# Key weights loaded in their natural layout and turned on TensorE, feature weights by rows, warm-ups between the first steps, and a new order of the first half, in a fused attention and Mish kernel

## Chip, cores and metric

One core of one Trainium2 chip runs the whole program. The metric is device time in microseconds, median of several executions. A profiled execution adds a trace of every engine: TensorE (PE, with its weight loads PEld), VectorE (DVE), ScalarE (ACT), GpSimd (POOL) and SyncE (SP), whose queue issues most DMAs.

## The reference

```python
def _A_ref(x, wqkv, w_phi, wo):
    B, S, D = x.shape
    H = 32; Dh = D // H
    qkv = (x @ wqkv).reshape(B, S, 3, H, Dh).transpose(2, 0, 3, 1, 4)
    q, k, v = qkv[0], qkv[1], qkv[2]
    pq = jnp.einsum("bhsd,hdf->bhsf", q, w_phi)
    pk = jnp.einsum("bhsd,hdf->bhsf", k, w_phi)
    phi_q = jnp.concatenate([_softmax(pq, axis=-1), _softmax(-pq, axis=-1)], axis=-1)
    phi_k = jnp.concatenate([_softmax(pk, axis=-1), _softmax(-pk, axis=-1)], axis=-1)
    kv = jnp.einsum("bhsf,bhsd->bhfd", phi_k, v)
    z  = jnp.einsum("bhsf->bhf", phi_k)
    num = jnp.einsum("bhqf,bhfd->bhqd", phi_q, kv)
    den = jnp.einsum("bhqf,bhf->bhq", phi_q, z)[..., None] + 1e-6
    return (num / den).transpose(0, 2, 1, 3).reshape(B, S, D) @ wo

def _B_ref(x, w1, b1, w2):
    h = jnp.einsum("bsd,df->bsf", x, w1) + b1
    sp = jnp.log1p(jnp.exp(-jnp.abs(h))) + jnp.where(h > 0, h, jnp.zeros_like(h))
    return jnp.einsum("bsf,fd->bsd", h * jnp.tanh(sp), w2)

xn = _layernorm(A_x, axis=-1)
return A_x + _A_ref(xn, A_wqkv, A_w_phi, A_wo) + _B_ref(xn, B_w1, B_b1, B_w2)
```

S is 2048 tokens, D 512, F 1792; 32 heads of 16. All inputs are bf16.

## The kernel before

Tokens are cut into 16 tiles of 128, four tiles to a group. A token tile is normalised (statistics `LS`, `LN`; root `RS`; centring `AZ`, `AP`), then turned so that features lie on partitions (xnT). The first group is turned on TensorE (`TP`, kept by `TC`), tile by tile; the others by DMA transposes on SP's queue.

The key projection and the feature weights w_phi are folded into one matrix: the key weights are turned (wT), multiplied by a block-diagonal form of w_phi (Wbd, made by `WB` from wsrc and the 0/1 pattern `block`), and the four products (`F0`) are copied into wkp (`FD`). wkp therefore holds first the natural key weights and then the folded ones. After it come logits (`LP` for the first two tiles, `L`, `WL`, copied by `LC`), values (`V`, `VC`), extremes (`E`), exponentials (`X`), sums (`S`), the reciprocals and products (`R`, `N`) and the accumulation of kv (`A`). The hidden layer of the Mish branch runs as 56 units `H` (four groups by 14 blocks of 128 features), each followed by its activation `M`. The second half has queries (`Q`, `G`, `C`), the second layer (`O`, `P`) and the output (`Y`).

Before, the key weights arrive in two ways: rows 0 to 255 by a natural load into wkp (L522), to be turned on TensorE by matmuls against the identity into fp32 banks (`TW`, L616; copied by `TK`, L622), and rows 256 to 511 by a transposing DMA straight into wT (L523). w_phi comes by a load whose runs are one row of 16 features long (L528). Twelve dummy matmuls (L554) run on TensorE before the first step.

The order of everything is written by hand as a string, STEPS, at line 24. Each step is a name with arguments; `@b` is the PSUM bank, `a`, `v` and `p` name ACT, VectorE or POOL. An engine runs its instructions in the order in which the steps issue them; a wait holds all that is behind it on that engine. There are six banks of 512 fp32, and a step that writes a bank waits until its last tile has been read. Mish on ACT uses another table than exponential and logarithm, so changing between them costs a table load (L139).

Of the kernel before, what the change touches and what calls it, by code (L numbers as in the profile page):

```python
# [8 lines left out]
BF16 = mybir.dt.bfloat16  # L9
# [3 lines left out]
ALU = mybir.AluOpType  # L13
# [15 lines left out]
2 @4; M 2; H 3 @5; H 4 @0; H 5 @2; VC 0 a; H 6 @1; M 3; M 4; M 5; H 7 @4; M 6; M 7; H 8 @3; H 9 @5;  # L29
H 10 @0; M 8; H 11 @2; H 12 @1; LN 1; M 9; E 0 0; AP 1 0; AP 1 1; H 13 @4; L 1 0 @3; DX 3; L 1 3 @5;  # L30
DW 2; E 0 1; X 0 1; LN 2; LC 1 0 v; LC 1 3 v; WL 1; LN 3; AP 2 0; AP 2 1; X 0 0; V 6 @3; M 10; M 11;
M 12; H 14 @5; S 0 0; WL 2; LC 1 2 a; VC 6 a; H 17 @2; H 16 @0; M 14; AP 3 0; AP 3 1; H 15 @3; M 17;
M 13; H 18 @1; M 15; H 20 @5; H 19 @4; M 20; LC 1 1 v; H 22 @2; M 16; WT; H 21 @0; M 18; H 26 @5; S
0 1; M 19; H 24 @3; H 27 @0; H 23 @5; M 21; M 26; H 25 @1; M 22; M 23; E 1 0; E 1 1; M 24; M 25; H
28 @4; H 29 @3; L 2 0 @2; M 28; L 2 1 @5; LC 2 0 v; M 27; F @4,3; L 2 2 @1; LC 2 1 v; M 29; R 0 0 a;
FC 1 v; FC 0 v; L 2 3 @0; FC 2 a; FC 3 a; L 3 0 @5; R 0 1 a; L 3 2 @3; V 7 @1; FT 0; LC 2 2 a; V 9
@0; FT 1; N 0 0; LC 2 3 v; X 1 1; E 2 0; V 3 @2; DW 3; X 1 0; A 0 0; VC 3 a; VC 9 a; L 4 0 @4; LC 3
0 a; V 2 @2; VC 7 a; V 8 @0; VC 8 a; VC 2 a; N 0 1; E 2 1; LC 4 0 v; L 3 3 @5; LC 3 3 a; LC 3 2 a; V
4 @0; A 0 1; VC 4 a; L 4 2 @1; X 2 0; V 11 @5; S 1 1; S 1 0; S 2 0; L 4 3 @3; VC 11 a; L 3 1 @0; L 4
1 @5; LC 3 1 a; LC 4 1 a; H 31 @0; LC 4 2 a; H 30 @5; V 5 @1; R 1 0 a; LC 4 3 v; M 30; VC 5 a; H 32  # L40
@4; M 31; M 32; R 1 1 v; H 33 @2; M 33; N 1 1; H 34 @1; H 35 @3; H 36 @5; M 34; H 37 @0; M 35; H 38
@4; E 3 0; H 39 @2; H 40 @1; M 36; N 1 0; M 37; M 38; M 39; H 41 @3; H 42 @5; H 43 @0; M 40; A 1 0;
M 41; E 3 1; M 42; M 43; A 1 1; X 2 1; V 12 @4; VC 12 a; L 5 0 @2; V 10 @1; V 15 @3; VC 15 a; V 13
@5; V 14 @0; E 4 0; E 4 1; LC 5 0 a; VC 13 v; VC 10 a; L 5 2 @4; X 3 1; X 3 0; L 6 3 @3; VC 14 a; L
5 3 @2; O 0 @5; LC 5 2 a; S 2 1; S 3 1; S 3 0; R 3 1 a; R 2 1 a; N 2 1; R 2 0 a; L 6 0 @1; R 3 0 a;
N 3 0; L 5 1 @0; LC 5 1 a; N 3 1; O 1 @4; L 6 1 @0; LC 6 0 a; LC 6 3 a; L 6 2 @1; H 44 @3; X 4 0; N
# [16 lines left out]
def kernel(  # L63
# [12 lines left out]
    nc = tc.nc  # L76
    P = 128
# [15 lines left out]
    wphi_v = A_w_phi.rearrange("(j i) a b -> (i a) j b", j=4)  # L93
# [18 lines left out]
    wsrc = wts.tile([P, 4, DH], BF16, name="wsrc")  # L112
    wv = wts.tile([P, KT, D], BF16, name="wv")
# [8 lines left out]
    ident = consts.tile([P, P], BF16, name="ident")  # L122
    mhalf = consts.tile([P, TPG], FP32, name="mhalf")
# [9 lines left out]
    tables = ["natural_log_exp_and_others"]  # L133
# [11 lines left out]
    pf_of = {}  # L145
# [28 lines left out]
    def centre(out, xs, mv, rstd):  # L174

        nc.vector.tensor_scalar(
            out=out, in0=xs, scalar1=mv[:, 0:1], scalar2=rstd, op0=ALU.subtract, op1=ALU.mult
        )
# [105 lines left out]
    def take(s, i, copy):  # L284
        if i == 0:
            p_of[s] = smx.tile([P, TPG, 512], BF16, name="p_sb")
        copy(p_of[s][:, i, :], pl_of.pop((s, i)))  # L287
# [229 lines left out]
    for t in range(2):  # L517
        nc.sync.dma_start(x_sb[:, t, :], x_v[:, t, :])


    wT_of = {0: lnp.tile([P, 4, 512], BF16, name="wT", tag="xn")}
    nc.sync.dma_start(wkp[:, 0:2, :], wqkv_v[:, 0:2, D : 2 * D])  # L522
    nc.sync.dma_start_transpose(  # L523
        out=wT_of[0][:, :, 2 * P : 4 * P], in_=A_wqkv[2 * P : 4 * P, D : 2 * D]
    )
    nc.scalar.dma_start(b1b[:], b1_v[:, :])
    with nc.allow_non_contiguous_dma(reason="tiny w_phi load"):
        nc.scalar.dma_start(wsrc[:], wphi_v)  # L528
    nc.sync.dma_start(x_sb[:, 2:4, :], x_v[:, 2:4, :])
    nc.sync.dma_start(wv[:], wqkv_v[:, :, 2 * D : 3 * D])  # L530
    nc.sync.dma_start(w1_sb[:, :, 0 : 7 * P], w1_v[:, :, 0 : 7 * P])
    nc.sync.dma_start(x_sb[:, 4:8, :], x_v[:, 4:8, :])
    nc.sync.dma_start(w1_sb[:, :, 7 * P : F], w1_v[:, :, 7 * P : F])

    nc.scalar.preload_act_table_set(tables[0])
    make_identity(nc, ident[:])

    nc.gpsimd.memset(block[:], 1.0)
# [6 lines left out]
    nc.gpsimd.memset(mhalf[:], -0.5)  # L545
    nc.gpsimd.memset(eps[:], 1e-5)
# [12 lines left out]
    for n in (512,) * WARM + (P,) * SHORT:  # L559
        dummy(n)  # L560

# [5 lines left out]
    def weights_by_block():  # L567
        nc.vector.tensor_tensor(
            out=Wbd[:].rearrange("p j (h e) -> p j h e", h=8),
            in0=block[:, None, :, :].to_broadcast([P, 4, 8, 16]),  # L570
            in1=wsrc[:, :, None, :].to_broadcast([P, 4, 8, 16]),
            op=ALU.mult,
        )
# [19 lines left out]
    def first_root(i, on):  # L593
        _, mv, rstd = ln_of[0]
        r = rstd[:, i : i + 1]
        if on == "a":
            nc.scalar.activation(r, mv[:, i, 1:2], ACT.Ln, bias=eps[:])
# [123 lines left out]
```

## Time and profile before

| | |
|---|---|
| Median of 3 runs | 173.83 us (173.5 to 173.9) |
| Profiled execution, its own time | 173.62 us |
| Span of the profile, first to last instruction | 171.9 us |
| TensorE busy | 168.3 us in 1047 matmuls |
| VectorE, ScalarE, GpSimd busy | 146.0, 122.2, 7.9 us |
| HBM read, written | 7.10 MB, 2.10 MB |

A line of a timeline has start, duration, engine, line, operation, tiles (out<-in), the number merged, and in brackets the idle time before it and what ended it. A line of the chain of waits has start, duration and the work that set the end at that moment. A DMA line has tiles, queue, number, size and the median time from issue to landing. A matmul's duration holds its way through the array, so the pace of a row of matmuls is read from the chain, where they do not overlap.

### The profile page before, as it was taken

What the parts mean: (1) busy time and instruction counts of PE and PEld (TensorE: products, weight loads), DVE (VectorE), ACT (ScalarE), POOL (GpSimd) and SP (SyncE); (2) the same over time, 40 slices, a digit from 0 to 9 for tenths busy, and PEclk for the clock granted to TensorE, in tenths of its full rate; (3) what the DMA queues carried; (4) which work ended last, traced back from release to release, by engine and by line L of the source; (5) the groups of instructions that cost most, each with busy time, mean ns of one, the idle gap of its engine ahead of it and who ended that gap; (6) DMA issues with size and microseconds to landing.
All of it is one profiled execution on the core that took longest, in us unless ns stands there. A gap on an engine that the chain in (4) does not pass through costs nothing.

```text
span 171.9 us, 2743 instructions
## 1 busy us (share of the span) xinstructions
PE 168.3 (98%) x1047; PEld 82.5 (48%) x1047; DVE 146.0 (85%) x226; ACT 122.2 (71%) x196; POOL 7.9 (5%) x23
## 2 busy tenths in 40 slices
PE   8999999999999999999999999999999999999993
PEld 3754444444445544454445644544444444554452
DVE  3769998999899999999989999899799998884333
ACT  2778899976998979799978989978282792432200
POOL 4122102300000000000000000000000000000000
PEclk9999999999999999999999999999999999999999
DMA  4997199686064000000000194309345628778641
GB/s 119 299 374 253 33 217 356 147 162 126 4 115 129 0 4 0 0 0 0 4 0 0 40 111 97 63 15 142 91 107 110 150 59 190 155 161 206 91 124 61
DMA packets 46297, 18.55 MB, mean 108 GB/s; under 512 B 38092, under 2 KB 46284, under 8 KB 46284
## 3 DMA queue, kind: packets, MB, share of 16 engines
q1 hardware_dynamic: 45584, 18.26, 45.8%
q10 hardware_dynamic: 700, 0.12, 0.4%
q8 instruction: 8, 0.13, 0.3%
q14 instruction: 5, 0.04, 0.1%
HBM read 7.10 MB, written 2.10 MB: 53 GB/s over the span
## 4 chain that ended last, share of the span: by engine, by line
PE 98%; DVE 0%; issue 0%
PE ph L263 28%; PE po L497 28%; PE pl L229 14%; PE po L504 8%; PE pv L229 8%; PE warm L554 3%; PE pnd L452 2%; PE pkv L421 2%; PE pl L244 1%; PE pwide L229 1%; PE pfold L151 1%; PE ptw L616 1%; PE ptr L609 1%; PE pfold L203 0%; DVE x_sb L511 0%; PE pb L577 0%
## 5 line engine op out<-in xcount | busy, mean ns | idle before, releaser
L497 PE MATMUL po<-w_sb,acts 128*128 128x512 bf16 (+2 forms) x238 | 50.8, 366 | 0.0
L263 PE MATMUL ph<-xnT,w_sb 128*128 128x512 bf16 x224 | 50.1, 379 | 0.0
L274 ACT ACTIVATE acts<-ph,b1f 128x512 bf16<-128x512 f32 x56 | 35.9, 694 | 5.4 <-PE ph L263 5.4
L340 DVE TENSOR_REDUCE s<-e 128x128 f32<-128x2048 bf16 x16 | 36.1, 2277 | 0.5 <-ACT e L323 0.5
L263 PEld LDWEIGHTS <-w_sb 128*128 128x128 bf16 x224 | 21.7, 98 | 25.9 <-issue 0.3
L497 PEld LDWEIGHTS <-acts 128*128 128x128 bf16 x238 | 22.1, 98 | 23.6
L323 ACT ACTIVATE e<-e 128x2048 bf16<-128x2048 bf16 x16 | 30.4, 1917 | 0.0
L229 PEld LDWEIGHTS <-xnT 128*128 128x128 bf16 x184 | 17.6, 98 | 20.3 <-issue 0.2
L511 DVE TENSOR_TENSOR x_sb<-po,x_sb 128x512 bf16<-128x512 f32 (+2 forms) x17 | 11.0, 656 | 8.4 <-PE po L504 8.4
L504 PE MATMUL po<-wqk,xnT 128*128 128x512 bf16 (+2 forms) x68 | 15.6, 366 | 0.0
L229 PE MATMUL pl<-wqk,xnT 128*128 128x512 bf16 x64 | 15.6, 379 | 0.0
L229 PE MATMUL pv<-wv,xnT 128*128 128x512 bf16 x64 | 15.4, 379 | 0.0
L287 ACT CAST p_sb<-pl 128x512 bf16<-128x512 f32 x21 | 11.9, 590 | 4.1 <-PE pl L229 4.0
L467 ACT COPY ds<-pnd 128x32 f32<-128x32 f32 x16 | 2.9, 183 | 16.5 <-PE pnd L452 16.5
L139 ACT ACT_TABLE_LOAD x10 | 12.8, 1283 | 0.2
L298 DVE TENSOR_TENSOR m<-m 128x512 bf16<-128x512 bf16 (+1 forms) x32 | 11.5, 358 | 1.1
L229 PE MATMUL pl<-wkp,xnT 128*128 128x512 bf16 x48 | 11.5, 379 | 0.0
L165 DVE BATCH_NORM_STATS2 stats<-x_sb 128x6 f32<-128x512 bf16 x16 | 10.1, 678 | 1.3 <-DMA x_sb<-in_A_x_dram 1.3
L298 DVE TENSOR_TENSOR m<-p_sb 128x1024 bf16<-128x1024 bf16 x16 | 10.9, 682 | 0.1
L307 DVE TENSOR_TENSOR e<-p_sb,m 128x2048 bf16<-128x2048 bf16 x8 | 9.8, 1225 | 0.4 <-PE pkv L421 0.2
L374 DVE TENSOR_TENSOR e<-e,r 128x2048 bf16<-128x2048 bf16 x8 | 9.6, 1219 | 0.6 <-ACT r L349 0.5
L307 DVE TENSOR_TENSOR e<-m,p_sb 128x2048 bf16<-128x2048 bf16 x8 | 9.8, 1226 | 0.3
(73 smaller groups left out, 134.0 us busy)
## 6 DMA issues: line engine op xcount, KB each, us to landing
w_sb<-in_B_w_dram SPq DMA_DIRECT2D x4, 896.0 KB, 8.0
out_dram<-x_sb SPq DMA_DIRECT2D x15, 128.0 KB, 2.0
x_sb<-in_A_x_dram SPq DMA_DIRECT2D x3, 512.0 KB, 8.0
wv<-in_A_wqkv_dram SPq DMA_DIRECT2D x1, 512.0 KB, 5.1
wqk<-in_A_wo_dram SPq DMA_DIRECT2D x1, 512.0 KB
x_sb<-in_A_x_dram SPq DMA_DIRECT2D x2, 128.0 KB, 2.1
wkp<-in_A_wqkv_dram SPq DMA_DIRECT2D x1, 256.0 KB, 3.5
x_sb<-in_A_x_dram SPq DMA_DIRECT2D x1, 256.0 KB, 3.5
```

Of the source, the lines that this page charges most:

```text
L139: nc.scalar.preload_act_table_set(name)
L229: nc.tensor.matmul(pp, lhsT=xnT[:, t, kt, :], rhs=w(kt), start=(kt == 0), stop=(kt == KT - 1),)
L263: nc.tensor.matmul(ph_of[u][:], lhsT=w1_sb[:, kt, f * P : (f + 1) * P], rhs=xnT[:, g * TPG : (g + 1) * TPG, kt, :], start=(kt == 0), stop= ...
L274: nc.scalar.activation(acts[:, f, g * 512 : (g + 1) * 512], ph_of.pop(u)[:], ACT.Mish, bias=b1f[:, f : f + 1])
L287: copy(p_of[s][:, i, :], pl_of.pop((s, i)))
L298: nc.vector.tensor_tensor(out=m[:], in0=src[:, :, 0:half], in1=src[:, :, half : 2 * half], op=op)
L307: nc.vector.tensor_tensor(out=e_of[s][:].rearrange("p t j l c -> p (t j) l c")[:, :, pl, :].rearrange("p t (c e o) -> p t c e o", e=8, o=2 ...
L323: nc.scalar.activation(v, v, ACT.Exp)
L340: nc.vector.reduce_sum(t[:], pair(s, k).rearrange("p t j l (c e) -> p (t j l c) e", e=16), axis=AX.X)
L497: nc.tensor.matmul(po_of[t, c.stop][:, c], lhsT=acts[:, f, t * P : (t + 1) * P], rhs=w2_sb[:, f, c], start=(f == 0), stop=False,)
L504: nc.tensor.matmul(po_of[t, c.stop][:, c], lhsT=oT_of[t // 2][:, t % 2 * 4 + j, :], rhs=wo_sb[:, j, c], start=False, stop=(j == 3),)
L511: nc.vector.tensor_tensor(out=y, in0=po_of.pop((t, c.stop))[:, c], in1=y, op=ALU.add)
```

## The change

The tables of the first steps are written anew, up to step `A 1 1`; behind it the order is the same, with other bank numbers. The parts:

- Both halves of the key weights come by natural loads into wkp (`D wn02`, `D wn24`), ahead of the second token tile in SP's queue; the transposing load is gone. All four quarters are turned on TensorE (`TW 0` to `TW 3`), by transposes into bf16 banks instead of matmuls into fp32 banks. `TK 0`, `TK 2`, `TK 3` copy on VectorE, `TK 1` on ACT.
- w_phi comes by rows, 128 bytes to a partition (wraw), and is spread to its place by 16 matmuls of 16 columns with a selector `sel` as weights (`WX`), which is then copied to wsrc (`WC`). The selector is written on VectorE and POOL into space that kvm uses later. The load is the first on ACT's queue, the bias load the second.
- `WB` runs on POOL instead of VectorE. Fills of ident, block, eps and mhalf are on VectorE instead of POOL.
- The twelve dummies become six of 512 and one of 64 columns, written as steps, and one of 64 behind the spread.
- In the order: statistics, roots and centring of tiles 0 to 3 lie between the turns; all four `FD` copies are on ACT; value tile 0 comes ahead of `LP`, which takes its two tiles one after the other; `V 1`, then `H 3`, `L 0 2` and so on; the load of the Mish table comes with `M 3`; `KM` comes behind `M 1`; hidden units, logits and values up to group 3 are in another order.

```diff
-WARM, SHORT = 9, 3
 STEPS = """
-KM; LS 0; RS 0 p; LS 1; RS 1 a; DX 2; PB @0; AZ 0; AZ 1; TW 0 @1; TW 1 @2; TP 0 @3; TP 1 @4; TK 0 a;
-TK 1 a; WB; F0 0 @5; FD 0 a; F0 1 @1; TC 0 v; F0 2 @2; F0 3 @3; FD 2 a; TC 1 v; FD 1 v; FD 3 a; LP i
-@4,5; LS 2; LS 3; RS 2 a; LC 0 0 a; V 1 @1; RS 3 p; AZ 2; TP 2 @2; TC 2 a; VC 1 a; AM; V 0 @3; LC 0
-1 v; AZ 3; CB; TP 3 @4; TC 3 v; L 0 2 @5; LC 0 2 a; H 0 @0; M 0; L 0 3 @2; LC 0 3 a; H 1 @1; M 1; H
...
+D x001 s; D phi a; D wn02 s; D b1 a; D wn24 s; D x011 s; TL; D x022 s; D wv s; D w10007 s; D x044 s;
+D w10714 s; DX 2; AW 512; AW 512; AW 64; AW 512; AW 512; LS 0; AW 512; AW 512; WX @3; AW 64; PB @5;
+TW 0 @2; WC v; CB; TW 1 @5; RS 0 a; WB p; AZ 0; TK 1 a; TP 0 @4; TK 0 v; TW 2 @1; LS 1; TW 3 @0; TK
+2 v; F0 1 @3; TK 3 v; F0 0 @5; TC 0 a; F0 2 @2; RS 1 a; FD 1 a; AZ 1; LS 3; F0 3 @4; LS 2; RS 3 p;
+TP 1 @1; FD 0 a; FD 2 a; FD 3 a; TC 1 v; RS 2 a; V 0 @3; AZ 3; LP t @0,2; TP 3 @5; AZ 2; TP 2 @1; LC
+0 0 a; V 1 @4; TC 2 v; TC 3 a; VC 0 a; LN 1; H 3 @5; L 0 2 @0; VC 1 v; H 6 @1; LC 0 1 a; LC 0 2 a;
+AP 1 0; L 0 3 @0; H 9 @3; H 7 @4; M 3; H 13 @2; LC 0 3 a; H 2 @0; M 9; H 1 @3; M 7; AP 1 1; E 0 0; M
+2; M 1; KM; H 5 @4; M 13; DX 3; H 4 @0; H 11 @5; M 5; DW 2; E 0 1; M 4; M 6; LN 2; M 11; WL 1; WL 2;
...
+    wraw = wts.tile([P, 4 * DH], BF16, name="wraw")
...
+    sel = kvm[:].rearrange("p k c -> p (k c)")[:, 0 : 4 * P + 4]
...
-    nc.sync.dma_start(wkp[:, 0:2, :], wqkv_v[:, 0:2, D : 2 * D])
-    nc.sync.dma_start_transpose(
-        out=wT_of[0][:, :, 2 * P : 4 * P], in_=A_wqkv[2 * P : 4 * P, D : 2 * D]
+    def load(what, on):
+
+        q = {"s": nc.sync, "a": nc.scalar}[on]
+        if what[0] == "x":
+            t = slice(int(what[1:3]), int(what[1:3]) + int(what[3]))
+            q.dma_start(x_sb[:, t, :], x_v[:, t, :])
...
+        elif what[:2] == "wn":
+            k = slice(int(what[2]), int(what[3]))
+            q.dma_start(wkp[:, k, :], wqkv_v[:, k, D : 2 * D])
...
+        elif what == "phi":
+            q.dma_start(wraw[:], A_w_phi.rearrange("h (c a) b -> (h c) (a b)", c=4))
...
+    nc.vector.memset(ident[:], 0.0)
+    nc.vector.memset(block[:], 1.0)
+    nc.vector.memset(sel, 0.0)
+    nc.vector.memset(eps[:], 1e-5)
+    nc.vector.memset(mhalf[:], -0.5)
+    nc.gpsimd.affine_select(
+        out=ident[:], in_=ident[:], pattern=[[-1, P]], compare_op=ALU.not_equal,
+        fill=1.0, base=0, channel_multiplier=1,
     )
...
-    make_identity(nc, ident[:])
...
+    nc.gpsimd.affine_select(
+        out=sel, in_=sel, pattern=[[1, 4 * P + 4]], compare_op=ALU.not_equal,
+        fill=1.0, base=-3, channel_multiplier=-4,
+    )
...
-    for n in (512,) * WARM + (P,) * SHORT:
-        dummy(n)
...
-    def weights_by_block():
-        nc.vector.tensor_tensor(
+    def spread(b):
+
+        pf_of["x"] = bank(b, "pspread")
+        for j in range(4):
+            for a in range(4):
+                nc.tensor.matmul(
+                    pf_of["x"][:, j * DH : (j + 1) * DH],
+                    lhsT=sel[:, j * P + 3 - a : (j + 1) * P + 3 - a],
+                    rhs=wraw[:, a * DH : (a + 1) * DH],
+                    start=(j == 0 and a == 0), stop=(a == 3), skip_group_check=True,
+                )
+
+    def weights_by_block(on):
+        {"v": nc.vector, "p": nc.gpsimd}[on].tensor_tensor(
...
-        ptw = pf_of["w", kt] = bank(b, "ptw")
+        ptw = pf_of["w", kt] = bank(b, "ptw", BF16)
         for j in range(4):
-            nc.tensor.matmul(
-                ptw[:, j * P : (j + 1) * P], lhsT=wkp[:, kt, j * P : (j + 1) * P], rhs=ident[:],
-                start=True, stop=True,
+            nc.tensor.transpose(
+                ptw[:, j * P : (j + 1) * P], wkp[:, kt, j * P : (j + 1) * P], ident[:]
             )
```

More of the change, by code (lines that the diff above doesn't have):

```diff
@@ L30 @@
[L30 to L34, printed above, removed]
@@ L600, in first_root, with first_apply @@
             root(r, mv[:, i : i + 1, :])
[L602 removed]
+    def first_apply(i, on="v"):
         _, mv, rstd = ln_of[0]
[L604 removed]
+        centre(
+            xn_of[0][:, i, :], x_sb[:, i, :], mv[:, i, :], rstd[:, i : i + 1],
+            {"v": nc.vector, "p": nc.gpsimd}[on],
+        )
     def first_turn(i, b):
@@ L667 @@
     run = {
-        "KM": masks, "AW": lambda: dummy(P), "WB": weights_by_block, "PB": bias,
+        "KM": masks, "AW": dummy, "WB": weights_by_block, "PB": bias, "WX": spread,
+        "WC": lambda c: copies[c](wsrc[:].rearrange("p j b -> p (j b)"), pf_of.pop("x")[:, 0 : 4 * DH]),
         "AM": lambda: table("mish"), "CB": lambda: nc.vector.tensor_copy(b1f[:], pf_of.pop("b")[:, 0:FT]),
```

96 lines of the change are left out of this document (48 added, 48 removed).

## The prediction

> **What bounds the kernel now.** First the page: the share of each engine and the clock row. Then the chain of waits in order of time, for where TensorE stands still.
>
> ```profile
> PE 168.3 (98%) x1047; PEld 82.5 (48%) x1047; DVE 146.0 (85%) x226; ACT 122.2 (71%) x196; POOL 7.9 (5%) x23
> ...
> PEclk9999999999999999999999999999999999999999
> ```
> ```profile
> 0.83 4.32 PE warm L554 x12
> 5.14 0.12 PE pb L577
> 5.27 1.01 PE ptw L616 x8
> 6.28 0.56 PE ptr L609 x8
> 6.84 1.02 PE pfold L151 x16
> 7.86 1.79 PE pl L244 x8
> 9.65 0.86 PE pv L229 x4
> ...
> 102.83 0.25 PE pnd L452 x8
> ...
> 168.89 0.24 PE po L504 x4
> ```
>
> TensorE is the bound, and each piece begins where the last one ends: from 5.14 to 169.13 us nothing else stands in the chain. So what follows the first folds (pfold) cannot get shorter by order alone. The change can win only by having useful matmuls done earlier than now, in the first eight us; it can lose anywhere.
>
> The clock row says full speed throughout, but the pieces say otherwise. Eight turns of the key weights (ptw) take 1.01, or 126 ns each; sixteen folds of the same 128 columns take 1.02, or 64 ns each. The turns of tokens between them (ptr, 70 ns) are a mixture. So TensorE ran at half speed until about 6.3 us, 5.5 us after its first matmul, with no gap in between.
>
> Next, the head in order of time (timeline), and from issue to landing (DMA view, first 20 us).
>
> ```profile
> 0.79 0.86 SPq L518 DMA_DIRECT2D x_sb<-in_A_x_dram  x2
> ...
> 1.58 0.75 POOL L540 TENSOR_SCALAR_AFFINE_SELECT block<-block 128x128 bf16<-128x128 bf16 x2
> ...
> 1.71 0.43 SPq L522 DMA_DIRECT2D wkp<-in_A_wqkv_dram  x1
> ...
> 2.18 1.33 SPq L523 DMA_TRANSPOSE wT<-in_A_wqkv_dram  x1
> ...
> 2.94 0.69 DVE L165 BATCH_NORM_STATS2 stats<-x_sb 128x6 f32<-128x512 bf16 x1 [0.35 <-DMA x_sb<-in_A_x_dram]
> ...
> 3.56 0.58 SPq L529 DMA_DIRECT2D x_sb<-in_A_x_dram  x1
> 3.67 0.18 DVE L167 BATCH_NORM_AGGREGATE mv<-stats 128x2 f32<-128x6 f32 x1
> ...
> 4.18 0.46 SPq L530 DMA_DIRECT2D wv<-in_A_wqkv_dram  x1
> ...
> 4.69 0.51 SPq L531 DMA_DIRECT2D w_sb<-in_B_w_dram  x1
> 4.74 0.29 ACT L597 ACTIVATE rstd<-mv,eps 128x1 f32<-128x1 f32 x1 [1.54 <-DVE mv L167]
> 4.87 0.85 DVE L176 TENSOR_SCALAR xn<-x_sb,mv,rstd 128x512 bf16<-128x512 bf16 x2 [0.23 <-POOL rstd L172]
> 5.07 0.20 ACT L598 ACTIVATE rstd<-rstd 128x1 f32<-128x1 f32 x1
> ...
> 5.63 0.42 DVE L568 TENSOR_TENSOR Wbd<-block,wsrc 128x512 bf16<-128x512 bf16 x1
> ...
> 5.89 1.07 ACT L622 CAST wT<-ptw 128x512 bf16<-128x512 f32 x2 [0.62 <-PE ptw L616]
> ...
> 6.65 0.75 DVE L628 COPY xnT<-ptr 128x512 bf16<-128x512 bf16 x2 [0.60 <-PE ptr L609]
> ...
> 7.10 1.65 ACT L160 CAST wkp<-pfold 128x512 bf16<-128x512 f32 x3
> ...
> 11.16 0.17 DVE L669 CAST b1f<-pb 128x14 f32<-128x14 bf16 x1
> ...
> 12.53 1.03 PE L263 MATMUL ph<-xnT,w_sb 128*128 128x512 bf16 x4
> ```
> ```profile
> w_sb<-in_B_w_dram SPq DMA_DIRECT2D x2, 896.0 KB, 9.8
> ...
> wv<-in_A_wqkv_dram SPq DMA_DIRECT2D x1, 512.0 KB, 5.1
> x_sb<-in_A_x_dram SPq DMA_DIRECT2D x2, 128.0 KB, 2.1
> wkp<-in_A_wqkv_dram SPq DMA_DIRECT2D x1, 256.0 KB, 3.5
> x_sb<-in_A_x_dram SPq DMA_DIRECT2D x1, 256.0 KB, 3.5
> ...
> wsrc<-in_A_w_phi_dram ACTq DMA_DIRECT2D x1, 16.0 KB, 3.9
> ```
>
> The first key weights land at 1.71 + 3.5 = 5.2, where the turns start; the value weights at 4.18 + 5.1 = 9.3, where the first value tile starts (timeline 9.49). My marker is the first hidden unit at 12.53. By then all turns and folds, two value tiles, the first logits (tiles 0 and 1) and L 0 2 are done.
>
> **The change part by part, against that marker.** I lay out the head anew on each engine, by these rows, in the new order.
>
> Loads. The 1.33 of the transposing load leaves SP's queue; a second natural load (0.43) enters, ahead of token tile 1. With a pitch of about 0.46, issues fall at 0.79 (tile 0), 1.25 and 1.7 (key weights), 2.2 (tile 1), 2.65 (tiles 2 and 3), 3.25 (value weights), with the rest behind them, w1's second half last at 4.85. First weights: between 1.25 + 2.1 = 3.35 (a tile in that place) and 1.25 + 3.5 = 4.75; I take 4.2, since it is double the tile's bytes. Tile 1 goes behind 512 KB of weights: 2.2 + 3.5 = 5.7. Value weights: 3.25 + 5.1 = 8.35, bounds 7.4 (the queue without the transposing read drains faster) and 9.3 (as now).
>
> Warm-ups. The twelve dummies are 4992 columns in 4.32. The new ones before the spread are six of 512 and one of 64, 3136 columns: 2.7, to 3.5.
>
> Spread (16 matmuls of 16 columns, new). No row shows one. The pnd row has 31 ns each for 68 columns at the full clock, ptw 126 ns at the half clock: 0.5 to 2.0 for the sixteen. Nearest is pnd at half clock, 62 ns: 1.0, so 3.5 to 4.5. It needs the feature weights: now one row per feature instead of 32-byte pieces, and issued first on ACT's queue, so no later than 0.79 + 3.9 = 4.7 and, by the tile row, perhaps at 2.9. It also needs the new selector on POOL: block's two selects took 0.75 for 128 columns each, four times that width at most 1.5, over by about 3. I charge no wait; at the late end it is 1.2.
>
> VectorE, in order: statistics 0 2.95 to 3.85; copy of the spread and bias copy (0.17 each) behind the spread, 4.7 to 5.1; centre 0 (0.41) to 5.5; copy TK 0 to 5.9; statistics 1 (0.87) to 6.7; TK 2 and TK 3 (0.35 each, as the two of L628 in 0.75) to 7.4; centre 1 to 7.8. **This queue sets the head**: behind it wait tile 1's turn and the last two folds.
>
> TensorE: bias and first turns 4.6 to 5.2, second turns to 5.7 (their bank waits for the bias copy), tile 0's turn to 6.2, third and fourth turns to 6.7, half of that at the full clock. The turns now number sixteen, not eight: 0.86 at half clock, the price of the load taken away, but TensorE would wait for VectorE anyway.
>
> Block-diagonal weights move from VectorE (0.42) to POOL. Bounds: 0.42, and 1.4 by four selects of 128 columns. I take 1.3: 4.9 to 6.2, still before 6.7, so it costs nothing; cover 0.5. The Trainium skill (GPSIMD Engine Reference, section 3.1) gives 2.6 cycles an element for two-input work, an estimate of 1.1 us and dispatch here; by that too it lies under the fourth turns.
>
> Folds 1, 0: 6.7 to 7.2; 2 behind TK 2, to 7.45; 3 behind TK 3, to 7.75. Tile 1's turn 7.85 to 8.1. All four key copies now stand on ACT (1.65 for three, so 2.2): 7.3 to 9.3; the first logits now take tile after tile, so the fourth is wanted at 9.6. It just hides. Then back to back: value 0 (0.86), first logits 1.79, two turns 0.45, value 1, H 3, L 0 2. From 8.1 this reaches H 6 at 13.75; with value 0 waiting for its weights until 8.35, at 14.0. H 6 has one more unit (0.86) behind it than the marker: 14.0 - 0.86 - 12.53 = **+0.6**.
>
> Reordering behind it. Its cover is ACT, six banks and the loads:
>
> ```profile
> L274 ACT ACTIVATE acts<-ph,b1f 128x512 bf16<-128x512 f32 x56 | 35.9, 694 | 5.4 <-PE ph L263 5.4
> ...
> L139 ACT ACT_TABLE_LOAD x10 | 12.8, 1283 | 0.2
> ```
>
> Thinnest is L 0 3: its bank is L 0 2's, whose copy (0.6) must end while H 6 runs (0.86), with ACT free then. The table load now falls on M 3 at about 14.8, so M 3 ends at 16.8; but TensorE has free banks until H 2 at 18.3, whose bank is free after LC 0 3 at 17.4. H 9 wants w1's second half at about 16, which lands at 4.85 + 9.8 = 14.7. Each unit costs TensorE 0.86 and ACT 0.69 or less. So I charge 0; TensorE having no slack, any wait there is lost in full. The mask (KM) moves to a later place on VectorE, 0.23 among extremes; free.
>
> Sum: span 171.9 + 0.6, and 1.72 outside it (173.62 - 171.9) make 174.2 for the profiled execution. That one lies 0.2 under the median of 173.83, so the forecast is **174.4**.
>
> **Rivals.**
>
> *The clock rises late.* Today's 5.5 us of unbroken matmuls are cut: 2.7 of dummies, then narrow matmuls, waits and turns, with folds from 6.7. If only dense matmuls count, the dummies keep their credit (2.8 more from 6.7: clock at 9.5) or lose it (5.5 more: 12.2). Half speed beyond 6.3 loses half of that, 1.6 to 2.9, less 0.3 of waits that it covers. I take the near end, since there is no long stop: 174.4 + 1.3 = 175.7; the far one is 177.0. For it: the new turns are transposes, the old were matmuls. Against: the old run's token turns were such transposes too, and the clock rose among them. The Trainium skill (TensorE: Matmul & The Clock Gate, Part 4) says that transposes do not count as busy the way matmuls do; by that rule this rival holds, while this trace cannot decide it, since by the means above only one or two of the eight token turns ran slow.
>
> *The loads come no earlier.* The bytes ahead of the value weights are the same as now. If these land at 9.3 and value 0, now first, waits: 1.2 over the 8.1 that I had, 0.6 over the forecast, 175.0.
>
> *Not slower.* The spread runs at 31 ns and VectorE never waits: centre 0 at 4.45, tile 1 landed by 5.2, centre 1 done at 7.1, tile 1's turn to 7.4, value weights there by 7.4 (the far bound). H 6 then starts at 13.0: -0.4, 173.4. It decides at value 0's start: below 7.75 the kernel is no slower. For it: 1.33 of SP's queue and 512 small packets are gone. Against: VectorE's queue is full even then.
>
> **How the numbers follow.** Chances: forecast 0.48, late clock 0.24, late loads 0.10, not slower 0.18. About 0.3% (0.5 us) can be told from no change. Half of "not slower" may pass -0.5 if several rows run short: faster 0.10. The forecast's own range, 173.8 to 175.0 by the bounds on loads and spread, lies below 174.35 for 0.4 of its chance: same 0.19 + 0.08 = 0.27. Slower is the rest, 0.63. The range runs from 173.3 (not slower) to 176.3: it leaves out the far end of the late clock and the best of the gain.
>
> **What would show it.** In the timeline: turns of the key weights from 4.6; folds from 6.7 at 64 ns; value 0 at 8.35 with a wait for its weights, or at 8.1 behind tile 1's turn; H 6 at 14.0 and no gap in the chain from there. Folds or value 0 at half pace (126 and 430 ns) mean the late clock. Value 0 after 9 means late loads. Wrong altogether: a gap between 14 and 60 us on TensorE, or the selector or POOL's product being what the folds wait for.

## The result, and the profile after

The changed kernel takes 176.62 us (median of 5, 176.37 to 177.06) against 173.57 for the kernel before on the same chip: ratio 1.018, interval 1.0164 to 1.0197. It is slower, as forecast, but by 3.05 and not by 0.6, and outside the range. The profiled execution took 176.37, its span 174.7, which is 2.8 more than before.

The page of the changed kernel: engines, the chain's shares, table loads, and key and value loads.

```profile
PE 167.3 (96%) x1051; PEld 82.3 (47%) x1067; DVE 146.9 (84%) x232; ACT 124.8 (71%) x201; POOL 7.7 (4%) x19
...
PE 72%; ACT 18%; DMA 6%; SPq 1%; issue 1%; DVE 0%; ACTq 0%
...
L140 ACT ACT_TABLE_LOAD x13 | 16.7, 1283 | 2.1 <-issue 1.9
...
wkp<-in_A_wqkv_dram SPq DMA_DIRECT2D x2, 256.0 KB, 3.0
wv<-in_A_wqkv_dram SPq DMA_DIRECT2D x1, 512.0 KB, 6.1
```

TensorE is no busier, and no longer the whole chain: ACT and two DMAs stand in it. The chain of waits in order of time names the DMAs:

```profile
3.22 6.08 DMA wv<-in_A_wqkv_dram
...
154.72 5.13 DMA qT<-e
```

**Head.** Its timeline (start, duration, engine, line, operation, tiles, and in brackets idle time and releaser):

```profile
3.39 0.62 PE L586 MATMUL pspread<-wraw,kvm 128*128 128x16 bf16 x16
...
4.43 1.30 DVE L177 TENSOR_SCALAR xn<-x_sb,mv,rstd 128x512 bf16<-128x512 bf16 x1
4.43 1.15 POOL L594 TENSOR_TENSOR Wbd<-block,wsrc 128x512 bf16<-128x512 bf16 x1 [1.45 <-DVE wsrc L698]
...
5.78 0.40 PE L639 MATMUL ptr<-ident,xn 128*128 128x128 bf16 x4 [0.85 <-DVE xn L177]
...
7.48 0.41 DVE L177 TENSOR_SCALAR xn<-x_sb,mv,rstd 128x512 bf16<-128x512 bf16 x1
...
7.95 0.40 PE L639 MATMUL ptr<-ident,xn 128*128 128x128 bf16 x4
```
```profile
9.35 1.04 PE L230 MATMUL pv<-wv,xnT 128*128 128x512 bf16 x3 [1.00 <-DMA wv<-in_A_wqkv_dram]
10.22 1.89 PE L245 MATMUL pl<-wkp,xnT 128*128 128x512 bf16 x8
11.95 0.61 PE L639 MATMUL ptr<-ident,xn 128*128 128x128 bf16 x8
12.39 1.03 PE L230 MATMUL pv<-wv,xnT 128*128 128x512 bf16 x4
13.26 1.03 PE L264 MATMUL ph<-xnT,w_sb 128*128 128x512 bf16 x4
14.12 1.03 PE L230 MATMUL pl<-wkp,xnT 128*128 128x512 bf16 x4
14.98 0.38 PE L264 MATMUL ph<-xnT,w_sb 128*128 128x512 bf16 x1
```

H 6 starts at 14.98; the same place was 12.53 + 0.86 = 13.39 before: **+1.59**. The folds ran at full pace, 56 ns from start to start (the 64 of the prediction is a mean that takes in a pause), with one stop of 0.33 in their middle. Then TensorE stood 1.0 us, because the first unit behind the folds is a value tile and its weights landed at 3.22 + 6.08 = 9.30. Before, the value weights landed at the same time (9.31), but logits started at 7.86 and covered that landing.

**Behind the head, +0.29.** From H 6's start to the accumulation of step `A 1` takes 61.48 us here, 61.19 before. Two pauses of TensorE are new, each 0.33 between weight loads where a steady row has 0.12 (0.216 from load to load, 0.098 of it busy). The old order has one, of 0.14 over the steady row, in that stretch. The timeline around both:

```profile
31.30 1.28 ACT L140 ACT_TABLE_LOAD   x1
32.03 2.10 PE L264 MATMUL ph<-xnT,w_sb 128*128 128x512 bf16 x8
...
32.59 1.84 ACT L275 ACTIVATE acts<-ph,b1f 128x512 bf16<-128x512 f32 x3
...
33.33 0.53 PEld L264 LDWEIGHTS <-w_sb 128*128 128x128 bf16 x3 [0.33 <-issue]
```
```profile
60.98 1.28 ACT L140 ACT_TABLE_LOAD   x1
...
65.86 0.57 ACT L254 CAST vext<-pv 128x512 bf16<-128x512 f32 x1
66.33 2.05 ACT L288 CAST p_sb<-pl 128x512 bf16<-128x512 f32 x4
...
66.97 0.96 PEld L230 LDWEIGHTS <-xnT 128*128 128x128 bf16 x5 [0.33 <-issue]
```

ACT loads a table 13 times, against 11 before (ten at L139 and the first one at L535), and runs without a break into both pauses: the activations and copies that free the banks come late.

**End, +0.85.** The timeline where the last turned queries are wanted:

```profile
156.01 1.32 SPq L331 DMA_TRANSPOSE qT<-e  x1
...
159.90 0.43 PE L453 MATMUL pnd<-kvm,qT 128*128 128x68 bf16 x8 [0.68 <-DMA qT<-e]
```

The two last transposes were issued at 154.72 and 156.01. In the DMA view of that stretch one 16 KB packet of another queue lies between them and their landing:

```profile
q1 hardware_dynamic: 1070, 0.27, 113.2%
q8 instruction: 1, 0.02, 3.3%
```

It is an instruction fetch, begun at 157.23; from 157.8 on 19 packets of the transposes take 1.5 to 1.9 us each. Before, the last fetch began at 159.44, behind those transposes (152.84, 154.15), and held stores only. The three parts make 1.59 + 0.29 + 0.85 = 2.73 of the 2.8.

### The profile page after: what moved, and what is told of

Read it like the earlier page. It is cut to its first block, busy times and chain, and to the rows that moved or that the text cites. A ratio compares the mean times of both kernels' runs of the same rounds, so it can differ in the third digit from the quotient of the medians.

```text
span 174.7 us, 2779 instructions
## 1 busy us (share of the span) xinstructions
PE 167.3 (96%) x1051; PEld 82.3 (47%) x1067; DVE 146.9 (84%) x232; ACT 124.8 (71%) x201; POOL 7.7 (4%) x19
## 4 chain that ended last, share of the span: by engine, by line
PE 72%; ACT 18%; DMA 6%; SPq 1%; issue 1%; DVE 0%; ACTq 0%
PE po L498 26%; PE ph L264 20%; PE pl L230 8%; PE po L505 7%; PE pv L230 6%; ACT acts L275 5%; ACT e L324 5%; ACT L140 4%; DMA wv<-in_A_wqkv_dram 3%; DMA qT<-e 3%; PE pnd L453 2%; ACT p_sb L288 2%; PE pkv L422 2%; PE pl L245 1%; SPq L525 1%
## 5 line engine op out<-in xcount | busy, mean ns | idle before, releaser
L264 PE MATMUL ph<-xnT,w_sb 128*128 128x512 bf16 x224 | 51.0, 379 | 0.1
L498 PE MATMUL po<-w_sb,acts 128*128 128x512 bf16 (+2 forms) x232 | 50.2, 366 | 0.3
L275 ACT ACTIVATE acts<-ph,b1f 128x512 bf16<-128x512 f32 x56 | 35.1, 701 | 3.5 <-PE ph L264 3.4
L288 ACT CAST p_sb<-pl 128x512 bf16<-128x512 f32 x27 | 15.2, 590 | 6.5 <-PE pl L230 5.3
L505 PE MATMUL po<-wqk,xnT 128*128 128x512 bf16 (+2 forms) x65 | 15.0, 366 | 0.2
L166 DVE BATCH_NORM_STATS2 stats<-x_sb 128x6 f32<-128x512 bf16 x16 | 10.1, 679 | 1.4 <-DMA x_sb<-in_A_x_dram 1.4
```

Source lines behind the costliest of these rows:

```text
L264: nc.tensor.matmul(ph_of[u][:], lhsT=w1_sb[:, kt, f * P : (f + 1) * P], rhs=xnT[:, g * TPG : (g + 1) * TPG, kt, :], start=(kt == 0), stop= ...
L275: nc.scalar.activation(acts[:, f, g * 512 : (g + 1) * 512], ph_of.pop(u)[:], ACT.Mish, bias=b1f[:, f : f + 1])
L498: nc.tensor.matmul(po_of[t, c.stop][:, c], lhsT=acts[:, f, t * P : (t + 1) * P], rhs=w2_sb[:, f, c], start=(f == 0), stop=False,)
L505: nc.tensor.matmul(po_of[t, c.stop][:, c], lhsT=oT_of[t // 2][:, t % 2 * 4 + j, :], rhs=wo_sb[:, j, c], start=False, stop=(j == 3),)
```

## The experiments

Each diff is against the changed kernel unless it says "before". "Stop" is TensorE's wait for the last turned queries; d is the begin of the last instruction fetch less the issue of the first of the last two transposes (before 6.6, changed kernel 2.5).

**1. Product back on VectorE.**

```diff
-WB p
+WB v
```


> The changed kernel with the block-diagonal product (WB) back on VectorE, all else as changed. In the changed kernel centre 0 (AZ 0) lasted 1.30 us beside POOL's product of 1.15, where the same instruction takes 0.41 alone, and the value weights landed at 9.30. Theory A (the value weights' landing is the gate of the head, since value 0 is the first dense work): centre 0 returns to about 0.41 and tile 0's turn comes 0.3 to 0.5 earlier, but value 0 still starts at 9.3, so the time stays within 0.2 us of the changed kernel. Rival B (POOL's product slowing VectorE is what costs the head): the head is 0.4 or more earlier and the time falls by as much. Either way, if the product also slows the loads (they fell from 350 to 240 GB/s in the half microseconds from 4.5 to 6.0), the value weights land before 9.0.

175.47 (ratio 1.0127, 1.009 to 1.0164), 1.15 better, where the first theory had 0.2 at most. VectorE's timeline shows both operations at their old lengths:

```profile
4.45 0.42 DVE L594 TENSOR_TENSOR Wbd<-block,wsrc 128x512 bf16<-128x512 bf16 x1
4.79 0.41 DVE L177 TENSOR_SCALAR xn<-x_sb,mv,rstd 128x512 bf16<-128x512 bf16 x1
```

The profiled execution was the slowest of the four (176.65): tile 1 landed late (6.67), H 6 started at 15.06 and the stop was there. So the slowing of centring is shown; where the faster executions won is not.

**2. Logits ahead of the first value tile.**

```diff
-V 0 @3; AZ 3; LP t @0,2; TP 3 @5;
+LP t @0,2; V 0 @3; AZ 3; TP 3 @5;
```


> The changed kernel with value 0 behind the first logits (LP), as the old order has it; all else as changed. Theory A (gate is the value weights): first logits start at about 8.4 when the copy FD 0 is out, and fill the wait; tile 1's logits then wait for its copy (TC 1, out at 9.8 behind statistics 3 and 2 on VectorE), so hidden unit H 6 starts about 0.3 to 0.4 us earlier and the time falls by that. Rival B (VectorE sets the head): no gain, within 0.15 us of the changed kernel.

176.3 (1.0139, 1.0101 to 1.0177). The wait for the value weights is gone (9.11, used at 11.04), and H 6 starts at 14.94 all the same: the logits began only at 8.76, behind folds that waited for their copies and behind the turn of tile 1. Inside the logits TensorE's weight loads then stand 0.82 for VectorE's copy of tile 1, which starts only at 9.72, behind the statistics of tiles 3 and 2. So VectorE's queue was the next gate behind the value weights. The stop remained (d 2.9), and the time cannot be told from that of the changed kernel: the two intervals overlap.

**3. Value weights ahead of tiles 2 and 3 in SP's queue.**

```diff
-D x022 s; D wv s;
+D wv s; D x022 s;
```


> The changed kernel with the load of the value weights ahead of that of token tiles 2 and 3 in SP's queue. Theory A: the value weights land 0.7 to 1.0 us earlier (8.3 to 8.6), value 0 starts there, and H 6 and the time come 0.6 to 0.9 earlier; tiles 2 and 3 land near 8, and statistics 3 starts there, which gives back 0.2 at most. If instead one of the sixteen rings runs late whatever its order, the value weights still land after 9.0 and nothing is won.

176.69 (1.0179, 1.0148 to 1.021). The weights land by 8.80, but tile 1 only at 7.34 and tiles 2 and 3 at 9.45: H 6 at 15.45. The order of the queue only moves the late one. No stop (d 3.0).

**4. Before, with its twelve dummies cut into more matmuls of the same columns** (33, 39 and 45 in all).

```diff
-WARM, SHORT = 9, 3
+WARM, SHORT = 2, 31
...
+WARM, SHORT = 0, 39
...
+WARM, SHORT = 33, 12
...
-    for n in (512,) * WARM + (P,) * SHORT:
+    for n in (P,) * WARM + (64,) * SHORT:
```


> The kernel before, with seven of its nine wide dummies cut into four of 128 columns each: the same 4992 columns, 21 matmuls and 21 weight loads more. Theory C (the last stop of the changed kernel, 0.85 us at the turned queries qT, comes from an instruction fetch for TensorE of 16 KB that now falls onto the transposing DMAs, because the change has 20 more matmuls with their loads): the last fetch moves from 159.4 to about 155, onto the qT transposes issued at 152.8 and 154.2, packets of these are held 1.5 us or more, and the kernel before gets a stop of 0.5 to 1 us near 157 with nothing else changed. Rival D (the stop belongs to the changed order): no stop, time within 0.2 us of the kernel before.

> The kernel before with all nine wide dummies cut into 128 columns: 27 matmuls and loads more than before. In the changed kernel the last fetch began 2.5 us after the issue of the first of the two last turned queries, and TensorE stopped; in the run with 21 more it began 3.2 after, caught only the tail of the second, and there was no stop. Theory C (the stop is the fetch's place against the transposing DMAs): the fetch now begins 1.9 to 2.8 after that issue, and TensorE stops 0.4 to 0.9 us before the last query tiles; the time is 0.3 to 0.9 above the kernel before. Rival D (it belongs to the changed order): no stop there.

173.89 and 174.14 (1.002, 0.9999 to 1.0042; 1.0028, 1.0011 to 1.0046). The last fetch moved from 159.44 to 156.59 and 155.91, d from 6.6 to 3.2 both times, and no stop came. For the third:

> The kernel before with its 12 warm-up matmuls (4992 columns) cut into 45 of the same columns (33 of 128, 12 of 64): 33 TensorE matmuls and 33 weight loads more ahead of everything, nothing else changed. Theory C (the stop at the last turned queries comes when an instruction fetch of 16 KB begins 2.5 to 2.9 us after the first of the last two turned-query transfers was issued, and the place of the fetch follows the count of TensorE's instructions before it): each 21 instructions or so have moved the fetch by about 3 us, from 159.44 to 156.59 with 21 more matmuls and to 155.91 with 27, so with 33 it begins at about 155, some 1.3 to 2.6 us after the first of the two issues; its packets hold the transposing packets for 1.5 to 2 us, TensorE stands 0.4 to 0.9 us ahead of the last query tiles, and the time is 0.3 to 0.9 above the kernel before. Rival D (the stop needs something of the changed kernel besides the fetch): a fetch in that window, no stop over 0.2, time within 0.3 of the kernel with 27 more (174.1). If the fetch begins outside of 1.3 to 2.9 us after the issue the run tells nothing of C against D.

174.29 (1.0051, 1.003 to 1.0071). The fetch began at 154.00, d 1.3, at the very edge of the stretch that the expectation names; the timeline of TensorE and the chain of this kernel:

```profile
157.83 0.36 PE L452 MATMUL pnd<-kvm,qT 128*128 128x68 bf16 x6 [0.65 <-DMA qT<-e]
```
```profile
152.69 5.10 DMA qT<-e
```

The stop of the changed kernel, in the kernel before, from nothing but 33 small matmuls and their weight loads 150 us earlier. So it needs none of the change's own parts.

**5. Natural second half of the keys alone** (before, with that part; its turns and copies added).

```diff
-    nc.sync.dma_start_transpose(
-        out=wT_of[0][:, :, 2 * P : 4 * P], in_=A_wqkv[2 * P : 4 * P, D : 2 * D]
+    nc.sync.dma_start(wkp[:, 2:4, :], wqkv_v[:, 2:4, D : 2 * D])
...
+TP 1 @4; TW 2 @5; TK 0 a; TK 1 a; WB; CB; TW 3 @0; F0 0 @1; FD 0 a; F0 1 @2; TC 0 v; TK 2 v; TK 3 a;
```


> One part of the change alone, in the kernel before: the transposing load of the second half of the key weights becomes a natural load in the same place of SP's queue, and two more turns (TW 2, TW 3, as matmuls into fp32 banks) with their copies (TK 2 on VectorE, TK 3 on ACT) are put in; the bias copy CB comes early to free its bank. Dummies, feature weights, token loads and the order behind the first logits stay as before. Theory E (the transposing load kept the sixteen rings together: behind it the next loads landed with 0.15 to 0.2 us between first and last ring, in the changed kernel with 1.1 to 2.4): tiles 2 and 3 or the value weights now land with over 1 us between first and last ring, and the value weights after 9.0 although they are issued 0.9 earlier. Rival F (the natural load is good by itself, and what hurts is the rest): value weights by 8.5. For the time: eight more turns at half speed cost 0.86, covered in part; 0.3 to 0.9 slower than before by E, within 0.3 by F.

174.63 (1.0054, 1.0036 to 1.0072): 0.95 comes with this one part. In its head the value weights, at 9.84, were not what TensorE waited for. It stood for the keys, which landed at 5.80 (before 5.20), and for the copy of an added turn; behind that the logits covered the value weights:

```profile
5.84 0.62 PE L616 MATMUL ptw<-ident,wkp 128*128 128x128 bf16 x8 [0.88 <-DMA wkp<-in_A_wqkv_dram]
...
8.75 0.40 PE L153 MATMUL pfold<-Wbd,wT 128*128 128x128 bf16 x4 [0.43 <-ACT wT L622]
8.98 1.89 PE L246 MATMUL pl<-wkp,xnT 128*128 128x512 bf16 x8
10.71 1.03 PE L231 MATMUL pv<-wv,xnT 128*128 128x512 bf16 x4
...
13.74 1.03 PE L265 MATMUL ph<-xnT,w_sb 128*128 128x512 bf16 x4
```

The first hidden unit starts 1.21 later than before (12.53). A load lands in sixteen pieces, one from each DMA engine; from first to last of them, in us:

```
kernel                   tiles 2, 3     value weights
before                   6.90 - 7.09    8.37 - 9.31
natural keys alone       5.94 - 8.40    7.73 - 9.84
changed                  5.42 - 7.02    7.28 - 9.30
changed, transposing     6.17 - 6.80    7.96 - 8.61
rows alone (below)       6.37 - 7.41    8.15 - 8.90
```

Without the transposing load the value weights are issued 0.96 earlier and their first piece lands earlier, but the last does not, and a user waits for the last. In the seven kernels here without that load, 1.8 to 2.3 us lie between the first and the last piece of the value weights, and the last lands at 9.1 to 9.8 (8.80 where they stand further ahead in the queue). In eight of the ten with it, the difference is 0.5 to 1.3 and the last lands at 8.6 to 8.9. The other two are the kernel before (0.94, 9.31) and the first of experiment 4, the same loads in the same order, where two of the sixteen pieces came 1.6 behind the rest (1.74, 10.03). So the pieces can drift apart with the load too, and one profiled execution fixes a landing only to about 1 us. Why they drift stays open.

**6. The changed kernel with the transposing load back.**

```diff
-D wn24 s
+D wt1 s
-TW 2 @1; TW 3 @0; TK 2 v; TK 3 v;
```


> The changed kernel with the transposing load back for the second half of the key weights, in the place of the second natural load; turns TW 2, TW 3 and copies TK 2, TK 3 left out. All else as changed (tile 1 behind the key weights, product on POOL, value 0 first, new order). Theory E: the loads behind it land with their rings together, the value weights still near 9.3 by the bytes ahead; VectorE loses 0.7 of copies, but tile 1 lands later (6.3 or more). So the time stays within 0.4 us of the changed kernel, since the gate is the value weights. Rival F (turning all keys on TensorE is what costs): 0.7 or more faster than the changed kernel.

175.12 (1.0089, 1.0057 to 1.0121), 1.5 better; "within 0.4" is refuted. The value weights land at 8.61 and value 0 starts 0.69 earlier than in the changed kernel (8.65 against 9.35), and there is no stop (d 6.4, 0.85). Another load takes part of that back: the first half of w1 lands only at 12.79 (11.63 in the changed kernel), so that the first hidden unit waits 0.28 and H 6 starts at 14.57, 0.41 earlier; the second half is waited for behind H 6, 0.34 more. 0.69 + 0.85 - 0.28 - 0.34 = 0.92 is what the profiled execution gained.

**7. That and the product on VectorE, without and with dummies in TensorE's waits.**

```diff
-WB p
+WB v
+AW 128; TP 0 @4; TK 0 v; LS 1; AW 128; AW 256; F0 1 @3;
```


> The changed kernel with two parts undone at once: the second half of the key weights loaded transposed again (its two turns and two copies left out), and the product for the feature weights on VectorE. Alone, the first took about 1.5 us off the changed kernel's time and the second about 1.15. If the two work at different gates (rings that land late; centring of tile 0 slowed beside the product) they add: 174.0 to 174.6, with H 6 starting near 13.9. If they open the same gate (the value weights' landing, or the stop at the end, which both moved), together they give no more than the better one alone: 174.9 to 175.3. In both cases the value weights land by 8.7, and the order behind the head still costs its 0.3.

175.62 (1.0148, 1.0095 to 1.02): neither theory's number. The weights landed at 8.64, as both had it, but H 6 started at 15.02. The clock was late: value tiles took 0.42 a matmul instead of 0.22, and the trace's record of the granted clock, which begins where matmuls reach full pace, begins at 10.14. With the last line of the diff:

> The changed kernel with both parts undone (second half of the key weights by the transposing load, product on VectorE), and three dummies (128, 128 and 256 columns) in TensorE's waits for the turn of tile 0 and ahead of the folds, where the granted clock of the version without them rose only at 10.14. Clock theory: the clock rises by 7, the value weights (8.6) are the next gate, and from there the same unbroken TensorE work as in the version with the transposing load alone follows (8.65 to 14.57), so the second hidden unit starts at 14.4 to 14.7, no stop at the end, time 174.7 to 175.2. Rival, that the head is held by VectorE or ACT and not by the clock and the landing: the second hidden unit at 14.9 or later, time 175.5 as without the dummies.

The clock came at 6.64 and H 6 started at 14.42, as the clock theory said. The time did not follow: 176.33 (1.0181, 1.0144 to 1.0218). Three matmuls more moved the last fetch from 161.09 to 156.77, d from 6.3 to 2.6, and the stop was back. From TensorE's timeline:

```profile
8.35 0.40 PE L641 MATMUL ptr<-ident,xn 128*128 128x128 bf16 x4 [1.03 <-DVE xn L179]
8.78 1.04 PE L232 MATMUL pv<-wv,xnT 128*128 128x512 bf16 x4
9.65 1.89 PE L247 MATMUL pl<-wkp,xnT 128*128 128x512 bf16 x8
...
14.42 1.03 PE L266 MATMUL ph<-xnT,w_sb 128*128 128x512 bf16 x4
```

Folds ended at 7.3, and the logits wait behind the turn of tile 1 and value tile 0 until 9.65. That is the order of the head and of its loads, with the other two parts undone.

**8. The change's parts with the old order of the rest, tile 1 ahead of the keys, product on VectorE, logits first; then with three dummies more behind the bias turn.**

```diff
+D x001 s; D phi a; D x011 s; D b1 a; D wn02 s; D wn24 s;
+PB @0; AW 512; AW 512; AW 128;
```


> A candidate: natural key loads, turns by transposes and feature weights by rows as changed, but token tile 1 loaded ahead of the key weights, the product on VectorE, statistics 1 and both centrings ahead of the copies, first logits ahead of value 0, and from there the order of the kernel before. By the rows: centre 1 done at 5.8 instead of 7.9, folds from 6.0, first logits from about 7.3 to 9.1, and L 0 2 at about 11.2 instead of 11.7: 0.3 to 0.5 us faster than before, if the value weights are not needed before 9.1 (in all runs so far they landed at 8.8 to 10.0, so they may take most of it back). If the late rings decide, it is within 0.3 us of the kernel before.

> The version with the change's parts, tile 1 ahead of the keys, the product on VectorE, logits first, and the old order of the rest (175.37), plus three dummy matmuls (512, 512 and 128 columns) behind the bias turn, where TensorE stood 1.17 us at 4.0 and the granted clock then stayed low until 9.92. Late-clock theory: the dummies hold the clock, it rises by 6.4, the folds of the feature weights take 0.8 rather than 1.6, and if the value weights (9.26 there) are not the next gate the time falls by 0.6 to 1.6, to 173.8 to 174.8. Rival: the rings are the gate (value weights at 9.0 or later), the clock rises early and the time stays within 0.3 of 175.37.

175.37 and 175.14 (1.0102, 1.0054 to 1.0149; 1.0103, 1.0071 to 1.0135). The clock came at 9.92 and, with the dummies, at 9.26: they did not hold it, since the keys landed at 5.6 and 6.5 and left a hole behind them. The second time is within 0.3 of the first, the rival's number, but not for its reason: the value weights (9.26 and 9.82) are not waited for, since the first value tile starts at 11.41 and 11.33, right behind the logits. The heads lose by the wait for the keys and by the late clock. Stop in the second (d 2.6), not in the first (3.0).

**9. A candidate: transposing load, value weights and both value tiles ahead of tiles 2 and 3, old rest.**

```diff
+D wt1 s; TL; D wv s; D x022 s;
+LP i @4,5; V 1 @1; V 0 @3; TP 2 @2; TP 3 @4;
```


> The head that the experiments point to: feature weights loaded by rows and spread on TensorE, warm-ups in the idle times, product on VectorE, tile 1 ahead of the keys, the second half of the keys by the transposing load behind the first, value weights ahead of tiles 2 and 3 in the queue, logits of slot 0 and values 1 and 0 ahead of the turns of tiles 2 and 3, and the old order of the rest. If value weights ahead of tiles 2 and 3 land by 8.0 and tiles 2 and 3 by 9.0, the first hidden unit starts 0.2 to 0.4 earlier than in the kernel before (12.53) and the time is 173.2 to 173.5. If the rings go apart as they did without the transposing load, values wait until 9 or later and the time is 174 or above.

175.19 (1.0102, 1.0085 to 1.0119). Folds start at 6.59, logits at 7.76 and values at 9.55, as before. But tiles 2 and 3 land at 9.70, and TensorE waits for both:

```profile
11.79 0.40 PE L641 MATMUL ptr<-ident,xn 128*128 128x128 bf16 x4 [0.34 <-DVE xn L179]
12.98 0.40 PE L641 MATMUL ptr<-ident,xn 128*128 128x128 bf16 x4 [0.80 <-DVE xn L179]
```

**10. Feature weights by rows alone: the old order of loads, head and rest; and the same with the new order behind the head.**

```diff
+D x001 s; D phi a; D x011 s; D b1 a; D wn02 s; D wt1 s; TL; D x022 s; D wv s;
+WX @3; AW 64; PB @0; AW 512; AW 512; AW 128; WC v; WB v;
```


> One part of the change alone: feature weights loaded by rows and spread on TensorE, with the warm-ups put into idle times, product on VectorE; the second half of the key weights by the transposing load, the order of loads, of the head and of all the rest as before. If this part costs nothing on the path (the folds wait for the transposing load, which lands near 6.3, not for the product): folds from 6.6, slot 0's logits from 7.7, value weights near 9.2 behind the logits, first hidden unit at 12.4 to 12.7, time 173.3 to 173.9. Rival (this part too drives the loads apart or delays the clock): value weights at 9.6 or later, or the clock past 7, and a time of 174.2 or above.

173.47 against 173.81 (0.9984, 0.9971 to 0.9997), so this part costs nothing and may be worth 0.3 us, less than the 0.5 that the prediction counts as a change. (With it go the turns by transposes into bf16 banks, the fills on VectorE and the root of tile 0 on ACT.) TensorE's timeline:

```profile
6.45 1.25 PE L154 MATMUL pfold<-Wbd,wT 128*128 128x128 bf16 x16
7.54 1.95 PE L247 MATMUL pl<-wkp,xnT 128*128 128x512 bf16 x8
9.33 1.03 PE L232 MATMUL pv<-wv,xnT 128*128 128x512 bf16 x4
...
12.37 1.03 PE L266 MATMUL ph<-xnT,w_sb 128*128 128x512 bf16 x4
```

> The kernel of the run beside this one (feature weights by rows alone, the head in the old order), with the changed kernel's order of everything behind the head; nothing else. If the new order itself costs what the changed kernel showed (61.48 from the second hidden unit's start to the second accumulation, where every version with the old order took 61.19), the span is 0.25 to 0.45 longer than that of its partner. Rival, that the 0.29 came with the changed head and not with the order: within 0.1 of its partner's span.

175.13 (1.0078, 1.0063 to 1.0094), and a span of 172.8 against 171.8: more than the 0.3 expected, and not the rival. From H 6 (14.00; its place in the partner is 13.23) to step `A 1` it takes 61.45 against 61.19: the 0.26 of the new order. The other 0.77 is a wait at the seam, in TensorE's timeline:

```profile
12.28 1.02 PE L266 MATMUL ph<-xnT,w_sb 128*128 128x512 bf16 x4 [0.61 <-DVE xnT L659]
```

A hidden unit needs all four turned tiles; put ahead of `L 0 2` it waits for the copy of the last one. In the changed kernel `V 1` stands between, and no such wait is there. The median lies 0.6 above the profiled execution; with d at 3.1 a stop in the others is possible, and not shown.

## Why the prediction missed

**What bounds, and where it can be lost: right.** "It can lose anywhere" held: all three losses are idle time of TensorE. For the profiled execution 174.2 was forecast and 176.37 measured. Of these 2.17, the value weights make 0.98, the order behind the head 0.29 and the stop at the end 0.85, 2.12 together.

**Spread, selector, dummies: right or too dear.** 1.0 forecast, 0.62 measured from the first start to the last end, and 27 ns from start to start. The part alone costs nothing.

**Loads: the failed term in the head.** Tile 1 (5.7, measured 5.80) and the first keys (4.2, measured 4.17) fit. The sign for late loads, value 0 after 9, came. The value weights, 8.35, landed at 9.30, which is the far bound and the condition of "the loads come no earlier". That rival had the right wait. Its reason, the same bytes ahead, is not enough: with the transposing load back the bytes are the same, and the weights land at 8.6. Its price was summed wrongly: with value 0 at 9.3 instead of 8.35, 0.95 comes over the forecast, not 0.6, so 175.35 and not 175.0. Measured, H 6 is 0.98 over the 14.0 forecast. The rest of the sum held: from value 0 to H 6 it has 5.65, and 5.64 was measured. The 5.1 from issue to landing was carried over from a kernel whose queue held that load; without it 6.1 was measured, and the pieces lie further apart. No row of one profile shows that, and the reason stays open.

**Product on POOL, "costs nothing; cover 0.5": the sum was right, the place wrong.** 1.15 against 1.3, and the folds did not wait for it. But beside it VectorE's centring took 1.30 instead of 0.41, which no term held. I asked who waits for the product, not whom it slows. The Trainium skill (GPSIMD Engine Reference, section 1) says that GpSimd shares its SBUF interfaces with VectorE and that some VectorE forms contend; the 1.30 of this trace fits that, but no run here tests which form does. What it costs in time stays open: 1.15 in the medians. With the transposing load back, H 6 starts at 14.57 with the product on POOL and at 14.42 with it on VectorE and three dummies more, and 0.28 of the 14.57 is the wait for w1, so that pair shows no cost at all.

**"This queue sets the head": half right.** VectorE was on time (centre 1 over at 7.9, forecast 7.8); behind it the value weights came last, and without that wait VectorE's copy of tile 1 is the next (experiment 2). The larger share of the 1.59 is the order that I took over without weighing it: the turn of tile 1 and value tile 0 stand ahead of the logits. With natural load and POOL product undone the place of H 6 is at 14.42; with the old order of head and loads besides, at 13.23. So, each from one profiled execution, some 1.2 belong to the order of head and loads, 0.56 to the natural load with the product (14.98 less 14.42, which is how much later value 0 starts), and the rows by themselves give 0.16 back. These shares hold for this order of undoing: in the old order the natural load by itself costs 1.21, at the turns of the keys (experiment 5). My sum had H 6 at 13.75 without any wait, 0.36 over the old 13.39, and did not ask what the order costs.

**"Reordering behind it: I charge 0": wrong, 0.26 to 0.29.** I checked banks and loads unit by unit and left ACT's table loads uncounted: two more at 1.28 us. The sign for "wrong altogether", a gap of TensorE between 14 and 60 us, came: the pause at 33.3. That these two table loads make the pauses is likely, since ACT runs through to both, but no run takes them out alone.

**The end: in no step.** That nothing behind the folds can get shorter was taken for: nothing there changes but the order. The stop of 0.85 needs only where an instruction fetch falls.

**The late clock** (chance 0.24) did not decide the profiled execution, whose clock came at 3.94. In three relatives with holes in the head it came at 9.3 to 10.1, so the rival was a real one. (In the kernel before, three of the eight token turns ran at half pace, 107 ns from start to start, and not one or two.)

## What to carry to other kernels

Look at the pieces of a load, not only at its bytes: what lands last gates its user, and taking a load out of a queue can change when the others land. Put work whose operands are there (logits) ahead of work that waits for a load (values). In a kernel with no slack, recount the instructions: a few dozen more on one engine can move a code fetch into a transpose that is waited for, 150 us later.

## What the runs showed of the hardware

- **Instruction fetch against transposes.** In the changed kernel a 16 KB fetch comes every 16 to 25 us. With d at 1.3, 2.5, 2.6, 2.7 and 2.9 TensorE stopped at the last query tiles; at 3.0 and above it did not, in any profiled execution; between 2.9 and 3.0 the line is thin. Its place moves in steps, not smoothly, with TensorE's instructions: 15 matmuls more than before (rows alone) left d at 6.2 in the old order, and brought it to 2.6 or 3.1 in the new one.
- **A product on POOL beside a centring on VectorE**: the centring took 1.30 instead of 0.41, and 0.41 as soon as the product moved.
- **The clock's rise.** Take the longest hole in TensorE's work between 4 and 6 us, from start to start of its matmuls less their pace (107 ns for 128 columns before the rise, 56 behind it). Of these seventeen kernels, the eight with at most 0.28 us had the rise at 5.4 to 6.6. Of the nine with 0.34 or more, six had it before the hole, at 3.9 to 4.6, and three only at 9.3 to 10.1. The changed kernel (3.94) and its version with both parts undone (10.14) run the same matmuls up to 4.2. The Trainium skill (TensorE: Matmul & The Clock Gate, Part 1) has a window of 3.4 us that runs freely of the kernel's start. The first rises, 3.9 to 6.6, spread over less than one such window, and the late ones less 3.4 fall at 5.9 to 6.7, in the same range: a window spoilt by the hole would do that. No run fixed the phase to test it.
